# Softmax mixture tail: combine weights of tiles 0 to 11 copied during expert 3, the slot sums in two parts

## The chip, the cores and the metric

The kernel runs on one core of a Trainium2 chip. The metric is device time in microseconds (us) for one execution. The kernel before was timed three times: 938.55, 940.98 and 941.99 us, a median of 940.98. The profiled execution is another one of the same kernel.

## What is computed

Attention with a window of 128 tokens (4 sequences of 576 tokens, 8 heads of 64) gives x, 2304 tokens by 512. A first mixture of four experts with given weights follows, and then a second, soft mixture of eight experts with four slots each. The change lies in the second one. Cut to what matters:

```python
def _moe2_ref(x, phi, w1, w2):          # x 2304 x 512, phi 512 x 32, w1 8 x 512 x 1024, w2 8 x 1024 x 512
    logits = x @ phi
    d = np.exp(logits - logits.max(0, keepdims=True))
    d /= d.sum(0, keepdims=True) + 1e-09
    slot_input = (d.T @ x).reshape(E, S_per_e, D)
    for e in range(E):
        slot_out[e] = np.maximum(slot_input[e] @ w1[e], 0.0) @ w2[e]
    c = np.exp(logits - logits.max(1, keepdims=True))
    c /= c.sum(1, keepdims=True) + 1e-09
    return c @ slot_out.reshape(n_slots, D)
```

d is a softmax over all 2304 tokens for each slot, c a softmax over the 32 slots for each token. slot_input needs every token, so no slot matmul can start before the last token tile is through.

## The kernel before

The 2304 tokens are 18 tiles of 128. The first mixture runs expert after expert. Its last expert, number 3, is done in six token groups (tiles 0 to 3, 4 and 5, 6 to 9, 10 and 11, 12 and 13, 14 to 17), each with two quarters of the hidden width (the loop at L979). L199 and L227 are its matmuls, L213 and L214 split its hidden values, and L237 adds its result to acc.

As soon as a tile is done, the loop puts the tail's work for it on a list, xq, with a number of steps to wait. x2_tile (L843) splits the tile into a high and a low half-precision part (L848 on ACT; L849 on POOL, on DVE for tiles 12 and up), and transposes both, by DMA for tiles 0 to 11 and on TensorE (L856, evacuated by L857 and L858) for 12 to 17. x2_log (L863) multiplies with phi (L869). For each of five groups of tiles (GR, L55: tiles 0 to 3, 4 to 7, 8 to 11, 12 and 13, 14 to 17) x2_l (L876) sums the logits into cm (L879), spreads them (L882), transposes them (L886) and takes the maximum (L887).

x2_d (L890) is the running softmax over tokens. It updates the running maximum (L902, L903), takes the exponential on ACT (L904), transposes it back (L908) and then, for the first four groups, multiplies it with the group's tiles of acc (sp, L935) and adds that to sacc, scaled by al, the correction for the new maximum (L937, L943). For the last group it forms al (L910) and a matrix w4 from it (L911), the high and low part dh of the exponential (L913, L914), and then sums in one PSUM tile, sip, for each of four chunks of 128: sacc times w4 (L918) and the last four tiles times dh (L921, twelve matmuls). L923 copies sip to siT, the input of the slots.

soft_c (L945) turns cm into the combine weights c, for tiles 0 to 11 and for 12 to 17 apart (L949 to L955). c_tr (L959) makes a half-precision copy of them, high part on ACT (L963), low part on DVE (L964), four tiles at a time, transposes it on TensorE (L968) and evacuates it (L970, L971). The copies are written into the two halves of dtb, which x2_d uses for its exponentials too.

After the last group the slots are computed in two halves of four experts: hp (L1040) is slot input times w1, evacuated at L1045, transposed at L1052, and so_ps (L1058) is the hidden values times w2. so2 (L1065, L1066) is its split, and L1071 multiplies the transposed c with it for the 18 output tiles.

The second mixture's weights are 64 loads of 512 KB in one fixed sequence, m2q (L772). pre (L788) issues the next ones of it into free buffers: 17 into the pool slb and two others on POOL's queue ahead of the loop (L973, L974), and 25 on ACT's queue during it and right after it (nine in x12 buffers, two behind each of four x2_d calls, eight at L1013). The rest go out on SP's queue: one at L1026, and one each time that a slot matmul has used up a buffer (refill, L805).

The order of each engine's queue is not written out. The program's order gives a rank, and a scheduler with a timing model of its own puts the instructions into the queues, taking the highest rank that is ready by its model. On the chip each queue runs in order.

## Time and profile before

| | us |
|---|---|
| median of three runs | 940.98 |
| lowest, highest | 938.55, 941.99 |
| profiled execution | 940.18 |
| its span, from the first to the last instruction | 938.3 |
| TensorE busy in the span | 886.7 (95%) |
| DVE, ACT, POOL busy | 566.5, 372.4, 179.9 |

The part of the page with forty slices (23.5 us each) shows where a busy TensorE is no longer the rule: it is busy nine tenths or more from the 12th slice to the 37th, and seven tenths in the 38th, which begins at 868 us and in which its granted clock is seven tenths too. The DMA engines, hardly used in the twenty slices before, are busy again from the 34th slice on, 774 us: eight, nine, eight, three, six, nine and six tenths. A row of the windows view gives a stretch, its length, the busy time of each engine with the instructions in it, the granted clock as a share of 2.4 GHz, the mean busy share of the 16 DMA engines, and what they moved. A row of the chain gives the start, the length, and the engine, tile and line that the end waited for at that time.

### The profile page before, as it was taken

What the parts mean: (1) busy time and instruction counts of PE and PEld (TensorE: products, weight loads), DVE (VectorE), ACT (ScalarE), POOL (GpSimd) and SP (SyncE); (2) the same over time, 40 slices, a digit from 0 to 9 for tenths busy, and PEclk for the clock granted to TensorE, in tenths of its full rate; (3) what the DMA queues carried; (4) which work ended last, traced back from release to release, by engine and by line L of the source; (5) the groups of instructions that cost most, each with busy time, mean ns of one, the idle gap of its engine ahead of it and who ended that gap; (6) DMA issues with size and microseconds to landing.
All of it is one profiled execution on the core that took longest, in us unless ns stands there. A gap on an engine that the chain in (4) does not pass through costs nothing.

```text
span 938.3 us, 16272 instructions
## 1 busy us (share of the span) xinstructions
PE 886.7 (95%) x6426; PEld 516.8 (55%) x6426; DVE 566.5 (60%) x1217; ACT 372.4 (40%) x912; POOL 179.9 (19%) x169
## 2 busy tenths in 40 slices
PE   4689898989899999999999999999999999999797
PEld 3566676656765655555555555555555445554432
DVE  7855565547549387657575756666666454556512
ACT  5956766757734243223131323232233201223412
POOL 5555655656520000000000000000000005310000
PEclk9989999999999999999999999999999999999799
DMA  9698998999960110100101010101001008983696
GB/s 261 124 192 157 178 191 174 185 199 152 147 142 24 46 46 3 44 23 23 45 1 45 1 46 1 45 3 44 23 23 46 0 1 303 221 216 133 237 377 241
DMA packets 222028, 102.35 MB, mean 109 GB/s; under 512 B 187216, under 2 KB 201584, under 8 KB 221952
## 3 DMA queue, kind: packets, MB, share of 16 engines
q1 hardware_dynamic: 212320, 78.14, 39.2%
q10 hardware_dynamic: 6800, 13.11, 4.0%
q0 software_dynamic: 2832, 10.07, 2.9%
q8 instruction: 50, 0.82, 0.4%
q14 instruction: 26, 0.21, 0.1%
HBM read 64.59 MB, written 4.72 MB: 74 GB/s over the span
## 4 chain that ended last, share of the span: by engine, by line
PE 75%; DMA 9%; ACT 4%; issue 4%; DVE 4%; POOL 2%; SPq 1%; POOLq 0%; DVEq 0%; ACTq 0%
PE l L709 22%; PE A L634 12%; PE l L199 9%; PE l L227 9%; PE C L634 6%; DMA eT<-e 4%; PE B L634 3%; PE hp L1040 2%; DMA qT<-qs 2%; PE l2f L276 2%; PE so_ps L1058 2%; PE x L402 1%; DMA m<-in_moe_w_dram 1%; ACT e L379 1%; PE fp L1071 1%
## 5 line engine op out<-in xcount | busy, mean ns | idle before, releaser
L709 PE MATMUL l<-w,h 128*128 128x512 f16 x1080 | 252.9, 379 | 0.0
L237 DVE SCALAR_TENSOR_TENSOR acc<-l,pr,acc 128x512 f32<-128x512 f32 x216 | 161.3, 748 | 126.6 <-PE l L709 103.3
L634 PEld LDWEIGHTS <-w 128*128 128x128 f16 x1260 | 123.1, 98 | 94.2
L709 PEld LDWEIGHTS <-h 128*128 128x128 f16 x1080 | 105.5, 98 | 115.3
L199 PE MATMUL l<-xT,w 128*128 128x256 f16 (+2 forms) x1152 | 149.4, 281 | 5.8 <-DMA xT<-xs 3.6
L227 PE MATMUL l<-w,h 128*128 128x512 f16 x600 | 141.9, 383 | 0.7 <-DVE acc L237 0.7
L658 ACT ACTIVATE ct<-A 128x384 f32<-128x384 f32 x90 | 43.5, 487 | 219.0 <-PE A L634 218.9
L199 PEld LDWEIGHTS <-w 128*128 128x128 f16 x1152 | 105.0, 99 | 39.4 <-issue 6.7
L803 POOL DMA_DIRECT2D m<-in_moe_w_dram x19 | 13.7, 723 | 510.2 <-DVE h L654 446.9
L385 POOL TENSOR_TENSOR e<-e,e 128x512 f16<-128x512 f32 (+1 forms) x72 | 80.9, 1130 | 61.8 <-ACT e L384 45.8
L227 PEld LDWEIGHTS <-h 128*128 128x128 f16 x600 | 57.8, 99 | 61.4 <-issue 3.5
L213 ACT ACTIVATE h<-l 128x256 f16<-128x256 f32 (+2 forms) x96 | 36.4, 382 | 110.2 <-PE l L199 75.9
L379 ACT ACTIVATE e<-e,nmx 128x256 f32<-128x256 f32 (+1 forms) x144 | 69.7, 485 | 20.2 <-DVE nmx L374 19.8
L214 DVE SCALAR_TENSOR_TENSOR h<-l,h 128x256 f16<-128x256 f32 (+2 forms) x96 | 40.9, 429 | 59.2 <-ACT h L213 59.0
L634 PE MATMUL C<-xs,w 128*128 128x384 f16 x360 | 71.3, 326 | 0.0
L374 DVE CUSTOM_DVE_ANT_0 e<-s,bias 128x256 f32<-128x256 f32 (+1 forms) x144 | 52.5, 404 | 28.4 <-PE s L362 23.5
L634 PE MATMUL A<-xs,w 128*128 128x384 f16 x360 | 69.3, 326 | 0.0
L634 PE MATMUL A<-xT,w 128*128 128x384 f16 x360 | 67.7, 327 | 0.0
L653 ACT ACTIVATE h<-ct 128x384 f16<-128x384 f32 x90 | 43.8, 515 | 46.5 <-PE l L709 25.1
L357 PE MATMUL s<-kT,qT 128*128 128x128 f16 x272 | 45.4, 228 | 7.7 <-DVE nmx L374 4.6
L654 DVE SCALAR_TENSOR_TENSOR h<-ct,h 128x384 f16<-128x384 f32 x90 | 47.6, 549 | 2.3 <-ACT h L653 2.1
L362 PE MATMUL s<-kT,qT 128*128 128x128 f16 x272 | 44.9, 230 | 4.0 <-DVE qT L342 4.0
(185 smaller groups left out, 993.2 us busy)
## 6 DMA issues: line engine op xcount, KB each, us to landing
m<-in_moe_w_dram ACTq DMA_DIRECT2D x25, 512.0 KB, 5.6
stg<-in_moe_w_dram SPq DMA_DIRECT2D x20, 512.0 KB, 4.9
m<-in_moe_w_dram SPq DMA_DIRECT2D x20, 512.0 KB, 10.2
m<-in_moe_w_dram POOLq DMA_DIRECT2D x19, 512.0 KB, 12.4
stg<-in_moe_w_dram SPq DMA_DIRECT2D x24, 256.0 KB, 3.2
out_dram<-ots SPq DMA_DIRECT2D x18, 256.0 KB, 3.0
qr<-in_q_dram SPq DMA_DIRECT2D x16, 256.0 KB, 3.9
kr<-in_k_dram SPq DMA_DIRECT2D x16, 256.0 KB, 4.3
```

The lines of the kernel that those rows point to most:

```text
L199: nc.tensor.matmul(pt, lhsT=w1_ap(e, fc, wa, kc), rhs=x_ap(t0, n, xa, kc), start=first_mm, stop=(kc == KC - 1 and wa == 1))
L227: nc.tensor.matmul(pt, lhsT=ht[:, ha, o:o + P], rhs=w2_ap(e, fc, wa), start=(fc == fcs[0] and ha == 0 and wa == 0), stop=(fc == fcs[-1] an ...
L237: nc.vector.scalar_tensor_tensor(out=a, in0=pt, scalar=p, in1=a, op0=ALU.mult, op1=ALU.add)
L357: nc.tensor.matmul(o, lhsT=qT[i][:, 0, h], rhs=mv, start=True, stop=False)
L362: nc.tensor.matmul(o, lhsT=qT[i][:, 1, h], rhs=mv, start=False, stop=True)
L374: nc.vector.tensor_tensor_reduce(out=et[:, hl, c0:], in0=st[:, hl, c0:], in1=bias[:, h, c0:], op0=ALU.add, op1=ALU.min, scale=-0.125, scal ...
L379: nc.scalar.activation(out=et[:, hl, c0:], in_=et[:, hl, c0:], func=AF.Exp, scale=-1.0, bias=nmx[i][:, h:h + 1], accum_out=sums[i][:, h:h ...
L385: nc.gpsimd.tensor_tensor(out=e2[:, :, 1], in0=et[:, :, c0:], in1=e2[:, :, 0], op=ALU.subtract)
L634: nc.tensor.matmul(o, lhsT=wq_[:, blk, wa, kc], rhs=xf(xa, kc), start=(first and kc == 0 and wa == 0 and xa == 0), stop=(kc == 1 and wa == 1),
L653: nc.scalar.activation(out=o[:, 0], in_=src, func=AF.Relu)
L654: nc.vector.scalar_tensor_tensor(out=o[:, 1], in0=src, scalar=0.0, in1=o[:, 0], op0=ALU.max, op1=ALU.subtract)
L709: nc.tensor.matmul(pt, lhsT=u["h"][:, z, ha, par, i * P:(i + 1) * P], rhs=w2_ap(e, 2 * qd + z, wa), start=(z == 0 and ha == 0 and wa == 0) ...
```

## The change

The combine copies of tiles 0 to 11 get two buffers of their own, cst, out of the pool slb, and that pool's prefetches go from 17 to 15. c_tr becomes three functions: c_prep (the copies), c_tp (the transposes) and c_ev (the evacuation). c_prep for the three groups of tiles 0 to 11 is put on the list xq behind soft_c, one step after another; c_tp for the three follows x2_d of the last group, each in a PSUM buffer of its own (X1, L2, L1); c_ev is held on ACT behind L913's instruction and on DVE behind the sum into siT. soft_c, the copies and the evacuations of tiles 12 to 17 are held in the same way.

In x2_d of the last group al and w4 come ahead of the exponential. sacc times w4 goes into a PSUM tile of its own, s0p, and is copied to siT; the last tiles times dh go into sip, and an add forms siT from both. x2_d of tiles 12 and 13 is taken out of the loop: it is due at 99 steps, and what is left on the list after the loop is sorted, so that what is due after more than two steps comes last. Its two prefetches move with it.

```diff
@@ -872,6 +872,7 @@
 
     lts = {}
     nruns = [0]
+    last = []
 
     def x2_l(g):
         t0, n = GR[g]
@@ -901,26 +902,32 @@
         else:
             nc.vector.tensor_tensor(out=new, in0=mg[:, g:g + 1], in1=old, op=ALU.max)
         nc.vector.tensor_scalar_mul(nmr, new, -1.0 / LS)
+        if g == NG - 1:
+            nc.scalar.activation(out=al, in_=old, func=AF.Exp, scale=1.0 / LS, bias=nmr)
+            nc.vector.tensor_scalar(out=w4, in0=sq4, scalar1=al, scalar2=DSC, op0=ALU.mult, op1=ALU.mult)
         nc.scalar.activation(out=dTt[:, 0:n * P].rearrange("p (j t) -> p j t", j=n), in_=lts[g][:, 0:n],
                              func=AF.Exp, scale=1.0 / LS, bias=nmr, accum_out=zg)
         dp = lts[g].rearrange("p j t -> p (j t)")[:, 0:n * NSL].rearrange("p (j s) -> p j s", j=n)
         for j in range(n):
             nc.tensor.transpose(dp[:, j], dTt[0:NSL, j * P:(j + 1) * P], ident[0:NSL, 0:NSL])
         if g == NG - 1:
-            nc.scalar.activation(out=al, in_=old, func=AF.Exp, scale=1.0 / LS, bias=nmr)
-            nc.vector.tensor_scalar(out=w4, in0=sq4, scalar1=al, scalar2=DSC, op0=ALU.mult, op1=ALU.mult)
+            s0p = ps.tile([P, KC, NSL], F32, tag="S1", name="s0p", bufs=1)
+            for kc in range(KC):
+                nc.tensor.matmul(s0p[:, kc], lhsT=sacc[:, kc * P:(kc + 1) * P], rhs=w4, start=True, stop=True)
+            nc.vector.tensor_copy(siT, s0p)
             dh = mp2.tile([P, 2, n, NSL], F16, tag="dh", name="dh", bufs=1)
-            nc.scalar.activation(out=dh[:, 0], in_=dp, func=AF.Copy, scale=DSC)
+            ahi = nc.scalar.activation(out=dh[:, 0], in_=dp, func=AF.Copy, scale=DSC)
             nc.vector.scalar_tensor_tensor(out=dh[:, 1], in0=dp, scalar=DSC, in1=dh[:, 0],
                                            op0=ALU.mult, op1=ALU.subtract)
             for kc in range(KC):
                 c = slice(kc * P, (kc + 1) * P)
-                nc.tensor.matmul(sip[:, kc], lhsT=sacc[:, c], rhs=w4, start=True, stop=False)
                 for j in range(n):
                     for xa, da in ((0, 0), (1, 0), (0, 1)):
-                        nc.tensor.matmul(sip[:, kc], lhsT=xl[t0 + j][:, xa, c], rhs=dh[:, da, j],
-                                         start=False, stop=(j == n - 1 and da == 1))
-            nc.vector.tensor_copy(siT, sip)
+                        mm = nc.tensor.matmul(sip[:, kc], lhsT=xl[t0 + j][:, xa, c], rhs=dh[:, da, j],
+                                              start=(j == 0 and xa == 0 and da == 0),
+                                              stop=(j == n - 1 and da == 1))
+            cp = nc.vector.tensor_tensor(out=siT, in0=sip, in1=siT, op=ALU.add)
+            last[:] = [z.ins for z in (mm, cp, ahi)]
             nc.vector.scalar_tensor_tensor(out=zacc, in0=zacc, scalar=al, in1=zg, op0=ALU.mult, op1=ALU.add)
             nc.vector.tensor_scalar_add(si, zacc, 1e-9)
             nc.vector.reciprocal(si, si)
@@ -956,21 +963,33 @@
 
     cT = []
 
-    def c_tr(g):
+    cst = {}
+
+    def c_prep(g):
         t0, n = CG[g]
-        c = nxt(dtb, 2).bitcast(F16).rearrange("p (h j a s) -> p h j a s", h=2, j=4, a=4)
+        if g % 2 == 0 and g < 4:
+            cst["t", g // 2] = sl([P, 2, 2, 4, 4, NSL], F16, "cst", slb)
+        c = cst[g] = cst["t", (g if g < 4 else 0) // 2][:, g % 2]
         src = cm[:, t0:t0 + n].unsqueeze(2).to_broadcast([P, n, 4, NSL])
         nc.scalar.activation(out=c[:, 0, 0:n], in_=src, func=AF.Copy)
         nc.vector.tensor_tensor(out=c[:, 1, 0:n], in0=src, in1=c[:, 0, 0:n], op=ALU.subtract)
-        cp = ps1.tile([P, 2, 4, P], F16, tag="X1", name=nm("cp"))
+
+    def c_tp(g, pool, tag):
+        t0, n = CG[g]
+        c = cst.pop(g)
+        cp = pool.tile([P, 2, 4, P], F16, tag=tag, name=nm("cp"))
         for hl in range(2):
             for j in range(n):
                 nc.tensor.transpose(cp[:, hl, j], c[:, hl, j].rearrange("p a s -> p (a s)"), ident16)
+        return cp
+
+    def c_ev(g, cp):
+        t0, n = CG[g]
         o = cT[t0 // 8][:, :, (t0 % 8) * P:(t0 % 8 + n) * P].rearrange("p a (j t) -> p a j t", j=n)
         nc.scalar.activation(out=o[:, 0], in_=cp[:, 0, 0:n], func=AF.Copy)
         nc.vector.tensor_copy(o[:, 1], cp[:, 1, 0:n])
 
-    pre(17, "slb")
+    pre(15, "slb")
     pre(2)
     xq = []
     GT = {GR[g][0] + GR[g][1] - 1: g for g in range(NG)}
@@ -991,9 +1010,11 @@
                     if t in GT:
                         xq.append([d, lambda g=g: x2_l(g)])
                         if g < NG - 1:
-                            xq.append([d + 3, lambda g=g: (x2_d(g), pre(2))])
+                            xq.append([99 if g == 3 else d + 3, lambda g=g: (x2_d(g), pre(2))])
                         if g == 2:
                             xq.append([d + 5, lambda: soft_c(0, 12)])
+                            for y in range(3):
+                                xq.append([d + 6 + y, lambda y=y: c_prep(y)])
                 for z in xq:
                     z[0] -= 1
                 for z in [z for z in xq if z[0] < 0]:
@@ -1002,7 +1023,7 @@
             hh.clear()
         if tl[-1] % TS == TS - 1:
             pre(1, "x12")
-    for z in xq:
+    for z in sorted(xq, key=lambda z: z[0] > 2):
         z[1]()
     si = mp.tile([P, 1], F32, name="si")
     w4 = mp.tile([P, NSL], F32, name="w4")
@@ -1013,16 +1034,20 @@
     pre(8)
 
     dq[0] = nc.sync
-    for g in range(3):
-        c_tr(g)
+    cps = [c_tp(0, ps1, "X1"), c_tp(1, ps2, "L2"), c_tp(2, ps, "L1")]
+    with tc.issue_after(last[1]), tc.issue_after(last[2]):
+        for g in (2, 1, 0):
+            c_ev(g, cps[g])
 
 
     so2 = sacc.bitcast(F16).rearrange("p (a d) -> p a d", a=2)
 
     def c_rest():
-        soft_c(12, NT - 12)
-        for g in (3, 4):
-            c_tr(g)
+        with tc.issue_after(last[1]), tc.issue_after(last[2]):
+            soft_c(12, NT - 12)
+            for g in (3, 4):
+                c_prep(g)
+                c_ev(g, c_tp(g, ps1, "X1"))
         pre(1)
 
     so_ps = ps1.tile([P, DM], F32, tag="X0", name="so_ps")
```

issue_after(i) makes each instruction of its block stand behind i in the queue of i's engine; it adds no wait of one engine for another.

## Rows read from the trace of the kernel before

**Rows 1.** Windows view: stretch, length, busy us (instructions) of each engine, clock, DMA.

```profile
core 0: us, PE busy (x) PEld busy (x) DVE busy (x) ACT busy (x) POOL busy (x), PEclk, DMA share, GB/s
776.00:866.00 90.00, 89.25 (x602) 48.17 (x601) 48.15 (x90) 22.50 (x48) 26.16 (x30) 1.00 0.75 220
866.00:878.80 12.80, 8.90 (x98) 5.32 (x97) 11.26 (x29) 7.43 (x16) 0.00 (x0) 1.00 0.92 331
878.80:889.00 10.20, 9.26 (x93) 6.14 (x96) 4.41 (x15) 3.97 (x9) 0.00 (x0) 0.50 0.45 159
889.00:895.80 6.80, 6.80 (x72) 2.41 (x68) 0.12 (x1) 1.86 (x3) 0.00 (x0) 1.00 0.75 242
895.80:916.00 20.20, 19.93 (x176) 6.45 (x172) 3.37 (x6) 1.65 (x3) 0.00 (x0) 1.00 1.05 399
```

**Rows 2.** Chain of waits, 866 to 886 us: start, length, what the end waited for.

```profile
871.27 0.60 DVE dtb L964
871.87 0.66 DVE sacc L943
...
878.29 0.26 DVE m__1324_9680 L952
...
878.62 0.14 DVE m__1324_9680 L953
...
878.84 0.79 ACT dtb L904 x2
...
879.67 0.44 PE lt L908 x2
...
880.19 0.64 ACT dtb L963
...
880.86 0.70 DVE dtb L964
...
881.60 0.61 PE cp L968 x4
...
882.48 0.45 PE sip L918 x2
...
884.80 0.85 PE cp L968 x8
```

**Rows 3.** Timeline of TensorE, first slot matmuls: start, length, instruction, idle before it.

```profile
885.58 8.74 PE L1040 MATMUL hp<-m,siT 128*32 128x512 f32 x64
...
886.44 0.20 PEld L1040 LDWEIGHTS hp<-m,siT 128*32 128x32 f32 x4 [0.66 <-issue]
...
889.43 0.12 PEld L1040 LDWEIGHTS hp<-m,siT 128*32 128x32 f32 x4 [0.31 <-issue]
```

**Rows 4.** Timeline of ACT and DVE at the last group's softmax and slot sums.

```profile
879.52 0.28 ACT L910 ACTIVATE al<-mrun,nmr 128x1 f32<-128x1 f32 x1
...
880.73 0.26 ACT L913 ACTIVATE dh<-lt 128x128 f16<-128x128 f32 x1
...
881.60 0.28 DVE L914 SCALAR_TENSOR_TENSOR dh<-lt,dh 128x128 f16<-128x128 f32 x1
...
884.84 0.29 DVE L923 COPY siT<-sip 128x128 f32<-128x128 f32 x1 [1.49 <-PE sip L921]
```

**Rows 5.** The weights' loads: issues on SP (page), first refill and last wait (timeline).

```profile
m<-in_moe_w_dram SPq DMA_DIRECT2D x20, 512.0 KB, 10.2
...
889.19 0.37 SPq L803 DMA_DIRECT2D m<-in_moe_w_dram  x1
...
918.55 0.27 PEld L1058 LDWEIGHTS so_ps<-m,hT 128*32 128x32 f32 x8 [0.59 <-DMA m<-in_moe_w_dram]
```

**Rows 6.** Timeline: update for tiles 12 and 13, and two batches of copy transposes.

```profile
867.63 0.47 ACT L904 ACTIVATE dtb<-lt,nmr 128x256 f32<-128x256 f32 x1 [0.28 <-PE l L227]
...
870.18 1.07 PE L935 MATMUL sp<-acc,dd 128*32 128x512 f32 x8
...
871.76 0.39 PE L968 MATMUL cp<-ident,dtb 128*128 128x128 f16 x4
...
872.20 0.39 PE L968 MATMUL cp<-ident,dtb 128*128 128x128 f16 x4
```

## The prediction, made before the changed kernel was run

> **What bounds the kernel now.** I began with the busy time by stretch [rows 1]. From 776 to 866 us TensorE is busy 89.25 of 90 us: expert 3 of the first mixture and the logits of the tiles that are done. Nothing that ACT, DVE or a queue saves there can shorten it. From 866 to 878.8 it is busy 8.90 of 12.80 us, so something else sets the pace, and from 878.8 to 889 its granted clock is 0.50, the lower of its two levels (1.2 instead of 2.4 GHz). From 895.8 to 916 two things are full at once: TensorE (19.93 of 20.20 us) and the DMA engines (share 1.05, 399 GB/s). After 920.4 come the output matmuls, which the change leaves alone. So only the stretch from 866 to 920.4 can answer, and the question is what ends last in it.
>
> For 866 to 885.6 that is told by the chain of waits [rows 2]. It runs through DVE and ACT: splits of the last tiles, logits, maximum, exponential, slot sums (sip), then the first slot matmul (hp, L1040) at 885.58. Eleven of its pieces belong to work that the change moves (L918 there three times, 0.45 us each). The first hp matmuls go four in 0.86 us and the later ones four in 0.43 us [rows 3]: the lower clock holds until 889.0.
>
> From then on the second mixture's weights must arrive. The profile has 20 loads of 512 KB on SP; the first that waits for an hp matmul goes out at 889.19, and the last one ends a wait of TensorE, 0.59 us at 918.55 [rows 5]. That wait is short, so TensorE and the loads end nearly together: an earlier start of hp pays only as far as the loads come earlier too.
>
> **The change part by part.** All minus signs are time saved on the chain to the first hp matmul.
>
> *The copies of tiles 0 to 11.* Six instructions (three on ACT, three on DVE) lose their turn on dtb and can run in expert 3. There TensorE covers them, and ACT is busy 22.50, DVE 48.15 of 90 us [rows 1], so six instructions of 0.6 to 0.7 us cost nothing; without that cover, three of DVE's could hold the sums into acc for 3 x 0.70 = 2.1 us. In the tail they leave the chain at two places. At 871.27 DVE's copy (0.60) goes. At 880.19 to 882.2 ACT's copy, DVE's copy and four transposes go: 0.64 + 0.70 + 0.61 = 1.95. What ran beside them comes up: dh high 0.26 and dh low 0.28 [rows 4], +0.54.
>
> *The update for tiles 12 and 13 put off.* Its sum into sacc (0.66 at 871.87) stood before the last tile's low half; with the copy, 1.26 is saved. Its other instructions move to a lower rank, and its two prefetches with them, on ACT's queue; they land before hp starts either way. Bounds: 0 if the update still goes where it went, 1.26 if it goes into gaps; I take 1.26, since DVE has 1.54 us free in 866 to 878.8 (12.80 less 11.26) and TensorE 3.90 [rows 1]. Both engines' gaps are fragments, so rival 2 prices the other outcome.
>
> *The second soft_c behind the slot sums.* Its two pieces between the maximum and the exponential go: 0.26 + 0.14 = 0.40. Behind hp's start it has hp's own 8.74 us [rows 3] as cover, and its transposes are due only at the output. The wait on ACT and DVE holds the evacuations of the three transposed groups; hp's second half needs their PSUM buffer only about 4 us later, so nothing behind them is late.
>
> *al and w4 moved up.* The 0.28 of al [rows 4] now stands on ACT ahead of the exponential: +0.28.
>
> *The sums apart.* Three pairs of L918 leave the chain at 0.45 each, -1.35 (the fourth ran beside ACT's copy). The four pairs, 1.80, now run beside the exponential (0.79) and dh (0.54), which leaves 0.47: +0.47. Bounds 0 and 1.80; the cover is in the rows, so I take 0.47. The sum siT is an add from PSUM like the copy before it: it costs 0.29 [rows 4], and since no transposes stand over it any more, +0.29.
>
> *The transposes.* The eight at 884.80 leave: -0.85. All 24 of tiles 0 to 11 are ready long before; their PSUM buffers come free when the last tiles are evacuated, around 870. If they fill TensorE's 3.90 us of gaps they cost 0; if they stand between sip and hp, 3 x 0.85 = 2.55, less the 0.29 of the add that they hide. I take 0, because TensorE's queue of before already took them among the last tiles once their input was there (four at 871.76 and four at 872.20) [rows 6]; the other end is rival 1.
>
> Sum: -1.26 - 0.40 + 0.28 - 1.95 + 0.54 - 1.35 + 0.47 - 0.85 + 0.29 = **-4.23 us**; hp would start at 881.35 instead of 885.58.
>
> *The clock takes part of it back.* If the lower clock again lasts to about 889.0, hp runs 4.23 us longer under it and loses half: +2.1. For TensorE alone the end comes 2.1 us earlier. Bounds: no lower clock at all under hp (rival 3) and this; I take this, because the gap before the exponential's transposes stays.
>
> *Two loads move to the end.* The two buffers for the copies come out of the prefetch pool, 17 to 15. POOL issues two loads fewer at 777 to 797, where the load has no effect on a full TensorE. But the sequence of 64 loads is unchanged, so two more are left for SP: 22 instead of 20 [rows 5]. A load is 0.524 MB, at 399 GB/s 1.31 us; two are +2.63 us behind the first refill. That refill follows the first 16 hp matmuls at the lower clock as before, so it comes 4.23 us earlier, and the loads end 4.23 - 2.63 = 1.6 us earlier. Bounds of the two loads: 2.63, or nothing if they fit into the share of 0.75 at 889 to 895.8, which leaves 1.7 us; I take 2.63, because there the queue had loads waiting and was no faster. The Trainium skill's "DMA: Bandwidth & Descriptors" (Where 436 GB/s comes from) says that a load from HBM is held to some 358 GB/s for a core, against a ceiling of 435 at the memory's ports; by 358 the two loads would be an estimated 2.93 us and the whole gain 1.3 instead of 1.6. The trace disagrees, 399 GB/s over 20 us, and the measurement decides.
>
> TensorE gains 2.1 and the loads 1.6; the later end counts: **-1.6 us**. The profiled execution took 940.18 us (span 938.3), so the sum gives 938.6; the median of the three runs is 0.8 above that execution, and against it the forecast is **939.4 us**. A measurement here tells apart from no change about 0.5%, 4.7 us (the three runs alone lie 3.4 apart): the forecast is no change that can be measured.
>
> **The rivals.**
> *1. The transposes stand last, between the slot sums and hp.* For it: the program has them exactly there, and nothing in hp's rank is lower. Against: TensorE has idle time while their input waits. hp then gains 4.23 - 2.55 + 0.29 = 1.97, the loads end 2.63 - 1.97 = 0.66 later: 941.6.
>
> *2. Slower: the put-off update becomes the late one.* Its place is after the last group's maximum: exponential 0.47, transposes 0.44, sp matmuls 1.07 and the sum into sacc 0.66 [rows 2, 6], 2.64 us in a row, and the first slot-sum matmul now waits for sacc, with sip behind it in TensorE's queue. It decides as soon as it takes more than 4.23 - 2.63 = 1.6 us of the gain, because the two extra loads then outweigh the rest. With all of it hp gains 1.59 and the loads end 2.63 - 1.59 = 1.04 later: 942.0. For it: the lowest rank in the list. Against: before, its exponential ran at 867.63 and its sp matmuls found a gap at 870.18 [rows 6].
>
> *3. The clock does not fall, or returns before hp.* The gaps of TensorE shrink when the chain is shorter. Then the first 16 hp matmuls take half of 4 x 0.86, 1.7 us less; the loads start 4.23 + 1.7 = 5.9 earlier and end 3.3 earlier: 937.7. Against: the clock fell after a stretch with TensorE busy 8.90 of 12.80 us, and the long wait for DVE and ACT in it stays.
>
> *4. The loads take all of the gain.* In 889 to 895.8 the DMA engines moved only 242 GB/s although loads were queued [rows 1]; if that slow start lasts 1.6 us longer with the earlier hp, the end stays where it was: 941.0.
>
> **How the numbers follow.** Forecast 0.48, rival 1 0.20, rival 2 0.12, rival 3 0.12, rival 4 0.08. The likeliest gives 939.4. The range takes in rivals 1 and 3, most of rival 2, and about 1 us to either side for the spread of a median: 936.6 to 943.3. To be faster by over 0.5% it must come under 936.3: rival 3 with the two extra loads hidden as well, TensorE alone, -4.23 - 1.7 = -5.9, 935.1; 0.05. Slower by over 0.5% is 945.7, which needs rivals 1 and 2 at once and more: 0.04. Within 0.5%: 0.91.
>
> **What would show it.** Right: the first L1040 at about 881 to 882; no copy of tiles 0 to 11 and no L952 between the last tile's split and the exponential; 24 transposes of the copies before the maximum of the last group; two loads fewer on POOL and 22 on SP, the first refill near 885; TensorE's waits on the weights in the last ten us before the output longer than 0.59 us in all. Rival 1 shows as 24 transposes in a block of 2.5 us ahead of L1040; rival 2 as L943 after L887 of the last group; rival 3 as a granted clock of 1.00 when hp starts. The prediction is wrong if hp starts 4 us earlier and the last load still ends no wait, or if the stretch up to 866 changes by more than 1 us.

## The result and the profile after

The changed kernel takes 946.02 us (median of seven runs, 943.77 to 947.09), the kernel before 940.98 (937.58 to 942.38, seven runs beside them): a ratio of 1.0052, 95% interval 1.0034 to 1.007. It is slower, by 5.0 us, where 939.4 was forecast. The profiled execution after took 943.77 us, span 942.0.

The windows view of the changed kernel, columns as in [rows 1]:

```profile
776.00:866.00 90.00, 86.17 (x572) 46.33 (x571) 46.28 (x86) 24.25 (x51) 24.70 (x28) 0.98 0.67 193
866.00:878.80 12.80, 11.51 (x109) 6.63 (x108) 9.63 (x20) 4.73 (x11) 0.00 (x0) 1.00 1.01 368
878.80:889.00 10.20, 6.88 (x94) 5.99 (x92) 4.02 (x14) 3.17 (x8) 0.00 (x0) 0.66 0.59 166
889.00:895.80 6.80, 6.42 (x57) 1.84 (x57) 4.00 (x12) 2.23 (x5) 0.00 (x0) 0.75 0.92 285
895.80:916.00 20.20, 20.20 (x175) 6.83 (x168) 2.00 (x4) 2.38 (x5) 0.00 (x0) 1.00 1.03 392
```

The first row is the news. Against [rows 1], TensorE has 3.08 us less busy time in 776 to 866 (86.17, 89.25 before) and 30 matmuls fewer (572, 602 before): the stretch that the prediction had called full is no longer full. What it waited for stands in two lines of the waits view of the changed kernel, TensorE, 776 to 866 us (total, times, longest). The kernel before has no line there at all.

```profile
PE lpb L869 <- DMA xtc<-xsc: 3.5, 1, 3.5
PE lpb L869 <- DMA xtb<-xsb: 0.2, 1, 0.2
```

So the logits of one tile, tile 9, waited 3.5 us for its DMA transpose. The timeline of the changed kernel, 822 to 838 us, shows what stood beside that transpose (start, length of the issuing, queue, line, transfer, count; a row with a count above 1 runs from its first issue to the end of its last):

```profile
822.83 1.23 SPq L860 DMA_TRANSPOSE xtb<-xsb  x1
823.37 0.96 ACTq L803 DMA_DIRECT2D m<-in_moe_w_dram  x2
824.18 10.30 SPq L860 DMA_TRANSPOSE xtc<-xsc  x2
824.40 2.25 ACTq L803 DMA_DIRECT2D m<-in_moe_w_dram  x3
...
836.19 0.41 PE L869 MATMUL lpb<-phi,xtc 128*128 128x64 f16 x8 [3.54 <-DMA xtc<-xsc]
```

And the same of the kernel before, 822 to 830 us:

```profile
822.34 1.23 SPq L860 DMA_TRANSPOSE xtb<-xsb  x1
823.84 1.23 SPq L860 DMA_TRANSPOSE xtc<-xsc  x1
826.57 2.47 ACTq L803 DMA_DIRECT2D m<-in_moe_w_dram  x5
```

The five loads are the same, two of x2_d's first call and three of the second x12 buffer. Before, they go out 2.7 us and more after the second of the two transposes shown (of tiles 8 and 9), which land 3.1 to 3.2 us after their issue; after, two go out ahead of tile 9's transpose and three right behind it. The DMA view gives the issues and the median time from issue to landing, for tile 9's transpose alone. The kernel before:

```profile
xtc<-xsc SPq DMA_TRANSPOSE x1, 3.1
```

The changed kernel:

```profile
xtc<-xsc SPq DMA_TRANSPOSE x1, 12.0
```

3.1 us became 12.0. The stall has a sequel, in a windows view of the changed kernel around it (columns as above):

```profile
832.60:836.20 3.60, 0.06 (x2) 0.02 (x2) 0.00 (x0) 0.63 (x1) 1.77 (x2) 1.00 1.00 212
...
837.70:841.10 3.40, 3.40 (x14) 1.81 (x12) 0.42 (x1) 0.21 (x1) 0.00 (x0) 0.51 0.00 0
```

After 3.60 us in which TensorE is busy 0.06, with the DMA engines full, the granted clock is 0.51 for 3.40 us: matmuls at 1.2 instead of 2.4 GHz, half of 3.4, 1.7 us lost. Together with the 3.08 that is 4.8 us of the 5.0 by which the last sum into acc comes later (table below).

The rest of the path is the chain of waits of the changed kernel, 866 to 890 us, which answers to [rows 2, 4, 6]:

```profile
874.75 0.40 PE xt L856 x4
875.14 0.45 PE cp L983 x8
...
877.13 1.00 PE sp L942 x8
878.13 0.55 PE cp L983 x8
...
878.80 0.46 PE xt L856 x8
...
881.90 0.96 PE lt L887 x4
...
882.88 0.70 DVE mg L888
...
883.99 0.30 ACT al L906
884.31 0.25 DVE w L907
...
884.70 1.89 PE s0p L916 x8
886.59 0.57 PE lt L912 x4
887.18 0.29 ACT dh L919
...
887.84 1.40 PE sip L926 x46
889.26 0.30 DVE siT L929
```

DVE's copies and soft_c are gone from it, as foreseen. In their place stand TensorE's own instructions: two batches of combine transposes (0.45, 0.55), sp of the put-off update (1.00) ahead of the last tile's transposes, and s0p (1.89). hp starts at 889.61, 4.0 us later than before. Of [rows 5], SP now has 22 loads. Two of them go out at 889.18 and 889.72, before an hp matmul has used up a buffer; the first that waits for one goes out at 892.90, 3.7 us later than before. The wait of so_ps on a load is gone. The loads on SP, from the page:

```profile
m<-in_moe_w_dram SPq DMA_DIRECT2D x22, 512.0 KB, 10.2
```

The table sets the traces side by side, one profiled execution each. The times are read from the timeline: end of the last matmul of L709 (work that the change does not touch), end of the last sum into acc (L237), start of the first hp matmul, end of the last so_ps matmul, span. In brackets the step from the column before.

| kernel | L709 ends | last acc | first hp | so_ps ends | span |
|---|---|---|---|---|---|
| before | 776.7 | 869.6 (92.9) | 885.6 (16.0) | 920.5 (34.9) | 938.3 (17.8) |
| after | 775.9 | 873.9 (97.9) | 889.6 (15.8) | 924.3 (34.7) | 942.0 (17.7) |
| 1: before, 15 loads | 777.1 | 874.0 (96.9) | 890.4 (16.4) | 925.2 (34.8) | 943.0 (17.8) |
| 2: five loads held | 777.9 | 872.8 (94.9) | 887.1 (14.3) | 922.0 (34.8) | 939.8 (17.9) |
| 3: and s0p later | 777.1 | 874.3 (97.2) | 889.2 (14.9) | 925.2 (36.0) | 943.0 (17.9) |
| 4: and no put-off | 777.8 | 872.8 (95.0) | 888.3 (15.5) | 923.3 (35.0) | 941.2 (17.9) |
| 5: nine loads held | 779.2 | 872.3 (93.1) | 884.1 (11.9) | 919.8 (35.6) | 937.5 (17.7) |
| 6: and sp, transposes later | 777.8 | 871.4 (93.7) | 882.9 (11.5) | 918.6 (35.7) | 936.3 (17.7) |
| 7: before, 15, held | 777.5 | 870.2 (92.7) | 886.4 (16.2) | 923.2 (36.8) | 941.0 (17.7) |
| 8: before, held | 778.4 | 871.3 (92.9) | 887.3 (16.0) | 921.5 (34.3) | 939.4 (17.9) |
| 9: two early, seven held | 778.7 | 871.5 (92.8) | 886.9 (15.5) | 922.5 (35.6) | 940.4 (17.9) |
| 10: three early, six held | 776.4 | 872.3 (96.0) | 884.2 (11.9) | 919.6 (35.4) | 937.4 (17.8) |
| 11: nine held, queue mended | 776.8 | 869.7 (92.8) | 880.4 (10.7) | 915.5 (35.1) | 933.2 (17.7) |
| 12: queue mended alone | 777.6 | 874.3 (96.6) | 887.2 (12.9) | 921.9 (34.7) | 939.6 (17.7) |

The loss of after stands in the second column, +5.0, and the gain that was forecast for the third, -4.2, is -0.2.

### The profile page after: what moved, and what is told of

Read it like the earlier page. It is cut to its first block, busy times and chain, and to the rows that moved or that the text cites. A ratio compares the mean times of both kernels' runs of the same rounds, so it can differ in the third digit from the quotient of the medians.

```text
span 942.0 us, 16270 instructions
## 1 busy us (share of the span) xinstructions
PE 888.5 (94%) x6426; PEld 518.2 (55%) x6426; DVE 567.7 (60%) x1218; ACT 372.5 (40%) x912; POOL 178.1 (19%) x167
## 4 chain that ended last, share of the span: by engine, by line
PE 73%; DMA 10%; issue 5%; ACT 4%; DVE 4%; POOL 2%; SPq 1%; ACTq 0%; POOLq 0%; DVEq 0%
PE l L709 22%; PE A L634 12%; PE l L199 9%; PE l L227 8%; PE C L634 6%; DMA eT<-e 4%; PE B L634 3%; DMA xtc<-xsc 2%; DMA qT<-qs 2%; PE hp L1065 2%; PE so_ps L1083 2%; PE l2f L276 2%; PE x L402 1%; ACT e L379 1%; PE fp L1096 1%
## 5 line engine op out<-in xcount | busy, mean ns | idle before, releaser
L709 PE MATMUL l<-w,h 128*128 128x512 f16 x1080 | 252.9, 379 | 0.0
L237 DVE SCALAR_TENSOR_TENSOR acc<-l,pr,acc 128x512 f32<-128x512 f32 x216 | 161.5, 748 | 120.3 <-PE l L709 103.3
L709 PEld LDWEIGHTS <-h 128*128 128x128 f16 x1080 | 105.7, 98 | 115.2
L199 PE MATMUL l<-xT,w 128*128 128x256 f16 (+2 forms) x1152 | 151.4, 282 | 5.7 <-DMA xT<-xs 3.4
L227 PE MATMUL l<-w,h 128*128 128x512 f16 x600 | 143.9, 384 | 0.0
L227 PEld LDWEIGHTS <-h 128*128 128x128 f16 x600 | 57.7, 99 | 59.3 <-issue 1.7
L213 ACT ACTIVATE h<-l 128x256 f16<-128x256 f32 (+2 forms) x96 | 36.4, 382 | 107.0 <-PE l L199 67.1
## 6 DMA issues: line engine op xcount, KB each, us to landing
m<-in_moe_w_dram SPq DMA_DIRECT2D x22, 512.0 KB, 10.2
```

The source lines that it names most:

```text
L199: nc.tensor.matmul(pt, lhsT=w1_ap(e, fc, wa, kc), rhs=x_ap(t0, n, xa, kc), start=first_mm, stop=(kc == KC - 1 and wa == 1))
L227: nc.tensor.matmul(pt, lhsT=ht[:, ha, o:o + P], rhs=w2_ap(e, fc, wa), start=(fc == fcs[0] and ha == 0 and wa == 0), stop=(fc == fcs[-1] an ...
L237: nc.vector.scalar_tensor_tensor(out=a, in0=pt, scalar=p, in1=a, op0=ALU.mult, op1=ALU.add)
L709: nc.tensor.matmul(pt, lhsT=u["h"][:, z, ha, par, i * P:(i + 1) * P], rhs=w2_ap(e, 2 * qd + z, wa), start=(z == 0 and ha == 0 and wa == 0) ...
```

## The experiments

**1. The kernel before with 15 early loads instead of 17,** nothing else of the change.

```diff
-    slb = ctx.enter_context(tc.tile_pool(name="slb", bufs=17))
+    slb = ctx.enter_context(tc.tile_pool(name="slb", bufs=15))
-    pre(17, "slb")
+    pre(15, "slb")
```

> The kernel before with 15 early loads on POOL instead of 17 (the pool shrunk to 15 buffers), nothing else. Theory A (two loads fewer on POOL let the first tiles' DMA transposes land some 3 us earlier, the model's order of the queues shifts, and the second set of five weight loads goes out on ACT's queue ahead of the transposes of tiles 8 and 9): TensorE again waits 3 to 4 us for xtc of tile 9 around 832 to 836 us, its clock falls for a while behind that, the last sum into acc ends 4 us later than before, and the time is 3.5 to 6 us above before, about 945. Theory B (the stall comes from the copies made during expert 3 or from the update put off): no wait of TensorE on a transpose above 0.5 us, and the time is that of before, 940 to 943 with two more loads at the end.

Measured: 946.91 us, ratio 1.007 (1.0051 to 1.0089). From the timeline of this run, 824 to 838 us:

```profile
824.67 1.23 SPq L860 DMA_TRANSPOSE xtb<-xsb  x1
825.21 0.98 ACTq L803 DMA_DIRECT2D m<-in_moe_w_dram  x2
826.01 10.64 SPq L860 DMA_TRANSPOSE xtc<-xsc  x2
826.25 2.16 ACTq L803 DMA_DIRECT2D m<-in_moe_w_dram  x3
...
837.28 0.41 PE L869 MATMUL lpb<-phi,xtc 128*128 128x64 f16 x8 [2.47 <-DMA xtc<-xsc]
```

The same five loads about the same transpose. So the whole loss comes with two loads fewer on POOL, a side effect of the buffers that the copies needed; not with the copies, the transposes or the sums. How the loss arises: the order of the queues has changed, and not only the times. In the kernel before the five loads stand together on ACT, from 826.57 on; here an L213 at 826.24 stands between the first two and the last three. As nothing else was edited, two loads fewer are what moved the scheduler's order; why by just this place is not shown.

**2. The changed kernel with these five loads held** on ACT behind the exponential of the second group.

```diff
-    xq.append([... lambda g=g: (x2_d(g), pre(2))])
+    xq.append([... lambda g=g: (x2_d(g), pre_d(g))])   # g = 0: none; g = 1: four, held
+    with tc.issue_after(held[1].ins):                  # the exponential of g = 1
+        pre(1, "x12")
```

> The changed kernel, with the five loads (two behind the update of the first group, three into the x12 buffer of tiles 6 to 11) held on ACT's queue behind the exponential of the second group, as they stood in the kernel before. Theory A: the wait for tile 9's transpose and the clock's fall behind it go, TensorE is busy 89 of 90 us again up to 866, and the time falls by 3.5 to 5 us to 941 to 942.5: no better than before, since the chain from the last sum into acc to the first slot matmul was 15.75 us against 15.96. Theory B: the stall stays or moves, 945 to 947.

Measured: 942.13 us, 1.001 (0.9991 to 1.0028). The two loads of the second group's own update were held with them. Four of the five us are back. What is left of the loss has moved to tile 11, in the timeline of this run, 832 to 850 us:

```profile
833.82 1.47 ACTq L803 DMA_DIRECT2D m<-in_moe_w_dram  x3
...
837.29 4.36 SPq L860 DMA_TRANSPOSE xtb<-xsb  x1
840.49 0.91 ACTq L803 DMA_DIRECT2D m<-in_moe_w_dram  x2
...
848.65 0.41 PE L869 MATMUL lpb<-phi,xtb 128*128 128x64 f16 x8 [1.58 <-DMA xtb<-xsb]
```

The held loads now stand about the next pair of transposes, of tiles 10 and 11, which land 8.3 and 11.3 us after their issue (3.6 and 3.2 in the changed kernel).

**3. Experiment 2, and the four s0p matmuls behind the exponential's transposes.**

```diff
+            with tc.issue_after(tr.ins):               # the last transpose of the exponential
                 for kc in range(KC):
                     nc.tensor.matmul(s0p[:, kc], ...)
```

> As the kernel with the held loads, and the eight matmuls of sacc times w4 stand behind the transposes of the last exponential in TensorE's queue. Theory C (those eight, 1.89 us at the lower clock, hold the transposes for 1.6 us): the transposes start within 0.1 us of the exponential's end, the first slot matmul comes 1.0 to 1.6 us earlier against the same point of the chain, and the time falls by 1 to 1.5 us below the kernel with the held loads. Rival D (the eight only change places and delay the slot sums instead, or the loads at the end take the gain): within 0.5 us of it.

Measured: 942.88 us, 1.0033 (1.0019 to 1.0046). The transposes follow the exponential 0.14 us behind it instead of 0.83, but the slot sums start 2.29 us behind the start of the transposes instead of 0.79. Of these 1.50 us 0.86 are the clock: s0p takes 1.91 us here and 1.05 in experiment 2, where the granted clock was still 1.00 at that time. The rest, 0.64, is what the transposes had won (0.69): the two change places, and nothing is won. That this trace is 2.3 us longer up to the last acc comes from the wait on tile 11's transpose (2.0 us instead of 1.6) and a granted clock of 0.50 for 3.4 us behind it, not from the edit.

**4. Experiment 2 without the put-off** of the update for tiles 12 and 13.

```diff
-    xq.append([99 if g == 3 else d + 3, ...])
+    xq.append([d + 3, ...])
-    for z in sorted(xq, key=lambda z: z[0] > 2):
+    for z in xq:
```

> As the kernel with the held loads, but the update of tiles 12 and 13 is not put off: it is due five steps later as before, and the list is not sorted. Theory E (the put-off update, with its sp matmuls and with eight copy transposes behind it, stands ahead of the last tiles' transposes in TensorE's queue and costs some 1.3 us there): the time from the last sum into acc to the logits of the last group falls from 7.1 to 5.5 to 6.4 us, total 0.5 to 1.5 us below the kernel with the held loads. Rival F (without putting it off, its sum into sacc comes back into the chain on DVE, 0.7 us): the same or up to 1 us slower.

Measured: 942.30 us, 1.0022 (1.0013 to 1.0032). From the last acc to the sum of the last logits (cm) it takes 7.16 us instead of 6.98: sp and sixteen transposes, in two batches of eight, still stand ahead of the last tile's. The rank that was changed is not what puts them there.

**5. The changed kernel with all nine loads held** that belong to the first three updates and to the second x12 buffer, behind the exponential of soft_c for tiles 0 to 11. In the changed kernel eight of them go out between 823 and 855 us, the ninth at 862.88 or later. Held, they go out from 845.34 us on, when no transpose is in flight.

```diff
+    def soft_ld():
+        ex = soft_c(0, 12)                             # returns its exponential
+        with tc.issue_after(ex.ins):
+            pre(1, "x12")
+            pre(6)
-    xq.append([... lambda g=g: (x2_d(g), pre(2))])
+    xq.append([... lambda g=g: (x2_d(g), pre(2 if g == 3 else 0))])
...
+        if tl[-1] % TS == TS - 1 and tl[-1] != 11:     # the second x12 call moves into soft_ld
```

> The changed kernel, with the nine loads that ACT issues between 823 and 855 us (two each of the first three group updates, three of the second three-row buffer) put behind the exponential of the combine softmax of tiles 0 to 11, so that none of them is in flight while the DMA transposes of tiles 8 to 11 run. Theory A (the loss is loads that are in the transposes' way): TensorE has no gap over 0.5 us on a DMA transpose, the stretch from the end of the last 512-column GELU-in matmuls to the last accumulate falls from 97.95 us to 92.9 to 93.4, the rest stays as in the run with five loads held (14.3 to 15.7 us to the first hp, 52.6 from there), so 160 to 161.5 us behind that point and a time of 938.5 to 941, ratio 0.998 to 1.0005. Rival B (loads put off come back at the end): the stretch is as short, but nine loads of some 1.35 us each land later, the last one more than 34.5 us behind the first hp instead of 33.3, so_ps ends 36 us behind hp instead of 34.7, and the time is 941.5 to 943. Rival C (the stretch is long for another reason, the order of the transposes of the moved work): it stays at 95 us or more without any gap on a DMA, and the time is 942 or more.

Measured: 938.07 us, 0.9963 (0.9947 to 0.9979), 8 us below the changed kernel. No wait on a transpose is left from 776 to 866 us, and the step to the last acc is 93.1. A part of B is true as well: the last load lands 34.3 us behind hp (33.3 in the changed kernel), and so_ps ends 1 us later behind hp. The third column came out better than expected, 11.9 instead of 14.3 to 15.7, with the same instructions; experiment 9 shows why.

**6. Experiment 5, with sp and the 24 combine transposes behind the last tile's logit matmuls.**

```diff
+    with tc.issue_after(lm[NT - 1].ins):               # last logit matmul; the same around sp for g == 3
         cps = [c_tp(0, ps1, "X1"), c_tp(1, ps2, "L2"), c_tp(2, ps, "L1")]
```

> The same with two things of TensorE's queue put behind the last tile's logit matmuls: all 24 combine transposes and the four sp matmuls of the update that the change puts off (in the changed kernel eight transposes, 0.62 us, and sp, 1.07 us, stand ahead of the last tile's own transposes). Theory A: the last group's logits come 1.2 to 1.7 us sooner, cm - acc falls from 7.0 to 5.3 to 5.8 us, the moved 2.9 us of TensorE's work lies in its wait for the logits' maximum, and the time is 1 to 1.7 us below the run without this, 937 to 939.8, ratio 0.996 to 0.999. Rival D: the update of the running sum now ends later, the four matmuls on it (s0p) wait for it and the slot sums start 1 us or more later than they would, so the way from the last accumulate to the first hp is no shorter than 14.3 us and the time equals that of the run without this within 0.5 us.

Measured: 937.70 us, 0.9955 (0.9942 to 0.9969). The sum of the last logits (cm) starts 3.39 us behind the last acc instead of 4.53, near A's gain; but sp and 16 transposes now stand ahead of the transposes of the last group's logits, and the maximum takes 3.13 us from there instead of 2.33. So 0.4 us of 1.14 reach hp, and by the median nothing that differs from experiment 5.

**7. Experiment 1 with the nine loads held,** and **8. the kernel before with the nine loads held.** The edit is that of experiment 5.

> The kernel before with 15 early loads instead of 17, and the same nine ACT loads put behind the softmax's exponential. Theory A: what the two missing loads cost (5.9 us in the run with 15 alone) is the loads' place among the transposes, so with them out of the way the stretch to the last accumulate is 92.9 to 93.4 us again and the two loads at the end cost 0.3 to 1 us: time 940.5 to 942, ratio 0.9995 to 1.0015. The price that I had put on the two loads at the end (2.63 us) would give 943.5, ratio 1.003. Rival C: the stretch stays over 95 us, ratio over 1.003.

> The kernel before, unchanged but for the same nine ACT loads put behind the softmax's exponential. It says what the late place of the loads costs or gains by itself. Theory A: no transpose waits in the kernel before, so nothing is gained in the stretch (92.9 us), and the loads land in time for the slots: time 940 to 942, ratio 0.999 to 1.001. Rival B: the last load lands over 1 us later behind the first hp than 32.9 us, ratio 1.002 or more.

Measured: 942.12 us, 1.0004 (0.9992 to 1.0015), and 941.34 us, 0.9999 (0.9985 to 1.0014). With the loads out of the way, 15 instead of 17 costs nothing up to the last acc (92.7), where it cost 4.0 in experiment 1. At the end it does cost: so_ps ends 36.8 us behind hp instead of 34.3, and 7 has a wait on the loads that 8 has not (waits view of experiment 7, 888 to 942 us, TensorE):

```profile
PE so_ps L1065 <- DMA m<-in_moe_w_dram: 0.8, 3, 0.3
```

By the traces so_ps ends 2.5 us later for two loads, and the last load lands 35.7 us behind hp instead of 32.3; by the medians it is 0.8. And 8 shows that holding the loads is worth nothing by itself.

**9. and 10. How many loads?** Experiment 5, with two loads (of x2_d's first call) or three (of the x12 buffer) left in their early place.

```diff
+    (x2_d(g), pre(2 if g in (0, 3) else 0))            # 9: two early, pre(4) held with the x12 buffer
+    if tl[-1] % TS == TS - 1: pre(1, "x12")            # 10: three early, pre(6) held
```

> The changed kernel with seven of the nine loads held behind the softmax, but the two of the first group's update left where the changed kernel has them (issued at 823.4 and 823.8 us there, just ahead of tile 9's transpose). It asks whether the wait goes by the number of loads. Theory A (the transpose lands when the loads about it have landed, 1.35 us each): in the changed kernel tile 9's transpose landed at 836.14 behind five loads, 3.5 us after TensorE was ready for it; three loads fewer give 836.1 - 4.0 = 832.1, before TensorE wants it, so no gap over 0.3 us on tile 9, 92.9 to 93.7 us to the last accumulate, time 937.5 to 940, as with all nine held (938.1). Rival F (any load issued beside a transpose holds it up by the whole of it, a matter of order and not of bytes): a gap of 3 us or more, time 941 or more.

> The same with six held and the three loads of the second three-row buffer left in their early place (issued from 824.4 us in the changed kernel, 0.2 us and more behind the issue of tile 9's transpose). Theory A, by number of loads: the transpose lands at 836.1 - 2 x 1.35 = 833.4 at the latest, a gap of 0 to 0.8 us, time 937.5 to 940.5. Rival F (order and not bytes): as these loads are issued behind the transpose, they hold it up by nothing at all: it lands 3.1 to 3.5 us behind its issue, as the transposes without loads do. Rival G (once loads are in flight, the transposes wait for all of them and for each other): a gap of 2 us or more and 941 or more.

Measured: 940.48 us, 0.9987 (0.9972 to 1.0002), and 942.60 us, 1.001 (0.9987 to 1.0033). Tile 9's transpose in the DMA view of experiment 9, and then of 10:

```profile
xtc<-xsc SPq DMA_TRANSPOSE x1, 6.0
```

```profile
xtc<-xsc SPq DMA_TRANSPOSE x1, 8.0
```

With the 3.1 of no load (as in experiment 5) and the 12.0 of five (11.2 and 11.7 in experiments 1 and 12) this is nearly a line: 2.9 us more for two, 4.9 for three, 8.1 to 8.9 for five, 1.5 to 1.8 us for each, little more than a load takes (1.31). Each of these is one profiled execution. So it goes by bytes, which speaks against F in both its forms: two loads do not cost what five do, and two of the three of experiment 10 were issued behind the transpose and held it up all the same. With two, TensorE does not wait (no line for it in the waits view). With three it waits 2.9 us, against my 0 to 0.8, which is what G gave: the transpose landed 0.5 us ahead of the second-last load, as A has it, but TensorE was ready at 829.4 instead of 832.6, so that I had the landing right and the need for it wrong. The runs of 10 lie from 936.1 to 946.5 us, those of 9 from 939.7 to 942.2.

Experiment 9 ends above A's 940 all the same: it has the tail of the changed kernel (15.5 us to hp), 5 and 10 one of 11.9. In 5 the last transposes of a tile (L856) end 3.0 us behind the last acc, in 9 and in the changed kernel 5.4: the scheduler has placed those of the earlier tiles further ahead among the matmuls of L227. Up to the sum of the last logits that makes 2.6 of the 3.6 us (4.53, 7.09). The other 1.0 is mostly the clock: in 9 it has fallen when s0p runs (1.88 us), in 5 not yet (1.05). All that differs in the program between 5 and 9 is the place of two loads.

**11. All nine held, sp as in 6, the 24 transposes behind the transposes of the last group's logits.**

```diff
+    with tc.issue_after(lt8[NG - 1].ins):              # last transpose into lt
         cps = [c_tp(0, ps1, "X1"), c_tp(1, ps2, "L2"), c_tp(2, ps, "L1")]
```

> All nine loads held, the four sp matmuls behind the last tile's logit matmuls, and the 24 combine transposes behind the transposes of the last group's logits (in the run before, 16 of them stood ahead of those and cost 0.8 us of the 1.14 us won). Theory A: logits' maximum 2.33 us after the last logits again, first hp 10.4 to 10.9 us behind the last accumulate (11.45 in that run, 15.96 in the kernel before); as the loads end the kernel from there, 0 to 0.8 us of it reach the time: 936.9 to 938, ratio 0.995 to 0.997. Rival H: the 24 transposes (1.9 us) now stand ahead of s0p and run into the exponential, so the first hp is no sooner than 11.4 us behind the last accumulate.

Measured: 937.47 us, 0.9969 (0.9955 to 0.9984). Its chain of waits, 869 to 890 us:

```profile
870.59 1.02 PE xt L856 x16
...
873.03 1.04 PE sp L945 x8
...
874.10 0.75 DVE sacc L953
874.85 0.61 DVE mg L890
...
876.58 1.05 PE s0p L918 x8
877.63 0.38 PE lt L914 x4
...
878.68 1.31 PE sip L928 x46
```

No combine transpose is left in it ahead of hp, and hp starts 10.7 us behind the last acc: the 24 transposes cost nothing in TensorE's wait for the exponential. s0p takes 1.05 instead of 1.89: the granted clock does not fall in this trace between 776 us and the end of the slots. The median does not move against experiment 6, the lower end of what A allowed. Why is not shown: A had the loads end the kernel, but in this trace they do not take the sooner hp back (the last one lands 34.0 us behind hp, 34.6 in 6, and so_ps ends 35.1 behind it instead of 35.7). The execution that was profiled is the fastest of the eleven, 935.01 us, so it does not tell what the others lose. The kernels of 5, 6 and 11 all beat the kernel before and the changed one; they are not told apart from each other.

**12. The changed kernel with only this edit of 11,** its early loads where it has them.

> The changed kernel with its early loads where it has them, and only TensorE's queue at the end mended: sp of the put-off update behind the last tile's logit matmuls, the 24 combine transposes behind the transposes of the last group's logits. Theory A (two losses that add up: loads among the transposes up to the last accumulate, and sp with 16 transposes ahead of the last tiles behind it): the gap on tile 9's transpose stays, 3 to 4 us, and 97 to 98.5 us to the last accumulate; the first hp comes 11 to 13 us behind that instead of 15.75; of these 3 to 4.5 us some reach the end, the rest is lost to the loads: 942 to 944.5, ratio 1.001 to 1.0035. Rival I (one cause: the late transposes also spoil the order at the end): the first hp stays at 14.5 us or more and the time at 945 to 947.

Measured: 942.84 us, 1.003 (1.0017 to 1.0043), inside A's bounds but for the step to the last acc (96.6, from 97). The first line of the waits view, TensorE, 776 to 866 us:

```profile
PE lpb L869 <- DMA xtc<-xsc: 3.7, 2, 3.2
```

The stall is there as in the changed kernel, the way from the last acc to hp is 12.9 us instead of 15.8. So the two losses can be had apart: 9 has the long tail without the stall, 12 the stall with a shorter tail. They do not add up to the last us: the tail of 12 is still 2.2 us longer than that of 11.

## Why the prediction was wrong

**The step that failed** is in the part on the two loads: "POOL issues two loads fewer at 777 to 797, where the load has no effect on a full TensorE", and with it the sentence that nothing on a queue between 776 and 866 us can matter. True of time saved there, it was taken for time lost too. Two loads fewer changed the scheduler's order of the queues, and five other loads came to stand about a DMA transpose that TensorE needs. In the changed kernel TensorE waited 3.5 us for the transpose and ran 3.4 us at half its clock behind that, and the last sum into acc came 5.0 us later behind the end of L709. Experiment 1 shows that this costs all of the loss and more (+6.3 us against the 940.58 of the runs beside it), experiments 5 and 7 that without the collision two loads fewer cost nothing up to the last acc (93.1, 92.7). I had named the test myself (a stretch up to 866 changed by over 1 us), but gave it no case and no price: the rivals all lay behind 866 us, so the range ended at 943.3. The trace of the kernel before would have given an estimate: the transposes and the loads are both there, and five loads one after the other, at the 1.31 us of the prediction, fill the 16 DMA engines for 5 x 1.31 = 6.6 us. The Trainium skill says in "DMA: Bandwidth & Descriptors" (Issuing engines are not separate DMA queues) that transfers started by different engines run on the same 16 DMA engines and interleave. The traces agree, with 3.1 us against 12.0.

**The way to hp** was to shrink by 4.23 us; it shrank by 0.2 in the changed kernel and by 0.5 in experiment 9, where the stall is gone. Step by step:
- *Copies, soft_c:* right; none of them is in the chain any more.
- *The update put off,* taken at -1.26: wrong. DVE is free of it, but sp (1.00 us on the chain) stands ahead of the last tile's transposes, and the sum of the last logits starts 7.1 us behind the last acc instead of 6.35. It is not the lower rank (experiment 4); the order that the scheduler finds is at fault (6 and 11 hold sp back by hand).
- *The transposes,* taken at 0: 1.00 us on the chain, two batches among the last tiles. My argument, that the queue took four of them at a time there before [rows 6], was no argument that they cost nothing there. Put behind the last logits' transposes, all 24 do cost nothing (11).
- *The sums apart,* taken at +0.47 for s0p behind its cover: mis-sized. s0p waits for w4, and w4 for the new maximum like the exponential: it starts 0.15 us before the exponential ends, and all of the rest of its 1.89 us (at the lower clock; 1.05 at the full one) is on the path, 1.74 instead of 0.47. dh was no cover either: it waits for the exponential's transposes, which stand behind s0p in TensorE's queue. Reordering does not help (3). sip itself is shorter than I took: 1.7 us from its first to its last matmul with dh, where 3.5 before, less the three pairs of 0.45, left 2.2.
- *al, siT:* 0.30 and 0.30, as taken.

**The clock** fell in the tail for 10.2 us as before, at 882.1 instead of 878.8, so hp ran 2.8 us under it (3.4 before), not 4.2 longer, as I had taken: the low stretch moved with the late tail. Rival 3, no lower clock under hp, is what the traces of experiments 11 and 12 show.

**The two loads at the end,** taken at 2.63 us: right in size in the traces of 7 and 8, where so_ps ends 2.5 us later behind hp (by the medians only 0.8), and without effect in the changed kernel, where hp started 4 us later and the loads had that much more time: the last one lands 33.3 us behind hp, 32.9 before. In 5 and 6 they take back a part, as rival 4 had it: the last load lands 34.3 and 34.6 us behind hp, and so_ps ends 0.7 and 0.8 us later behind it than before.

So the idea of the change is sound: without the collision and with TensorE's queue in order hp starts 5.3 us sooner behind the last acc (10.7, 16.0 before), where I took 4.23. A part of these 5.3 is the clock, which the prediction left as it was up to hp and which does not fall in that trace; on s0p alone it is 0.84 us. At the end 0.3 to 0.5% of the time is left (ratios 0.9969 and 0.9955 of 11 and 6). In 5 and 6 the account closes to about half a us: of 4.1 and 4.5 us won up to hp 0.7 and 0.8 go to the loads, and the medians are 3.1 and 3.5 us under the kernel before. In 11 it does not: its steps from L709 on are 5.2 us shorter, its median 3.9 us, and where the difference goes is open.

## What to carry to other kernels

When a change moves or drops a transfer, ask not only what waits for that transfer but which queues are planned anew because of it, and look for DMA transposes with weight loads issued within a few us of them. A stretch in which an engine is full has no time to gain but much to lose, so it needs a rival of its own. Prefetches that nothing needs for tens of us are best tied behind an event by which the last transpose has landed, and work that only has to be done some time behind an instruction after which the engine is known to wait.

## What the hardware showed unexpectedly

A DMA transpose of a tile (128 x 1024, half precision) lands 3.1 us after its issue when it is alone, 6.0 and 8.0 with two and three loads of 512 KB about it and 11.2 to 12.0 with five (three traces), the last of them issued up to 1.7 us behind it. And one gap of 3.6 us in a TensorE otherwise full was followed by a granted clock of 0.51 for 3.4 us, which began 1.5 us after the work had come back. The gap of 2.0 us in experiment 3 was followed by such a stretch too, those of 2.5, 2.9 and 3.2 us in 1, 10 and 12 were not; what decides it is open.
